# Another order for the loading phase of a fused cross-read and gated feed-forward kernel

## The chip, the cores and the metric

The kernel runs on one core of a Trainium2 chip. The metric is the device time of one execution in microseconds (us); the time of a kernel is the median of its runs. The names of the engines are those of the profile: PE is TensorE, DVE is VectorE, ACT is ScalarE, POOL is GpSimd, SP is SyncE. Each of them takes its own queue of instructions in order. DMAs are issued from the queues of POOL, SP and ACT, and 16 DMA engines carry them.

## What is computed

`x` has 8 batches, 8 heads, 512 tokens and 64 columns; `state` has 8 batches, 8 heads, 32 rows and 64 columns. Each reads the other by softmax attention; the results stand beneath each other, 544 tokens of 512 columns (the heads side by side) for each batch, and go through a gated feed-forward layer with 1536 inner columns:

```python
a = softmax(x @ state.T / 8)            # 512 x 32 for each head
xread = a @ state
a2 = softmax(state @ x.T / 8)           # 32 x 512 for each head
sread = a2 @ x
y = concat([xread, sread], axis=2)      # -> (8 * 544, 512), heads side by side
out = (sigmoid(y @ w_gate) * (y @ w_val)) @ w_out
```

Inputs and output are float32. The kernel multiplies in bfloat16 and sums in float32.

## The kernel before

**Algebra.** `xread @ w` is `a @ (state @ w)`, so the kernel never makes `xread`. For each batch it multiplies the 256 state rows (8 heads of 32) with the gate and value weights: `SW` (2 halves of 128 rows, gate and value, 1536 columns). Then `gv_mm(b, f)` (L340, its matmuls at L348) makes the gate and the value of 128 inner columns for the batch's 512 tokens: two matmuls each, `SW` times the transposed, normalised scores `aT`. `gv_th` (L354) is the tanh on ACT that stands for the sigmoid, `gv_glu` (L363) the product on DVE, `out_mm(b, k)` (L373, matmuls at L379) a third of the output product of 128 tokens. The `sread` rows of all batches are collected in `XS` and make a ninth, last "batch" of 256 rows.

**Scores.** `S_mm` multiplies transposed x (`xT`) with transposed state, `S_exp` is the exponential on ACT (the scores are small, no maximum is taken), `n_sum` and `n_mul` normalise half a batch on DVE, `n_sums` and `n_muls` a whole one (L159, L165). `aT` comes from PE for batches 0 and 1 (`aT_mm` L212, copied by `aT_cp`), from four DMA transposes on SP for the others (`aT_dma` L228). `xT` likewise: `xT_mm` (L110) with `xT_cp` on PE for batches 0 and 1, four DMA transposes (`at_xT_dma` L121) for the others, which read `xb`, the bfloat16 copy of x in another order that `cast_x` (L97) makes. `at_Eb` (L145) casts the exponentials on POOL for the `sread` side, and `sr_mm`, `sr_fin`, `p_tok`, `p_fold` make the `sread` rows of the first three batches.

**State.** `load_s(0)` brings the states of batches 0 and 1 in float32, `load_sb(q)` (L424) those of batches 2q and 2q+1 by a casting DMA, for q = 1 to 3. `sT_mm(q)` (L432) transposes them on PE: for q = 0 by eight matmuls with the identity into 64-row halves of the result, for q = 1 to 3 by eight matmuls with half the columns of the identity, one for each pair of an upper or lower half `e` and a quarter `l`. `sT_cp` brings the result to `sTc`, `sT_pad` and `pad` bring it beside zeros (`sTd`, `sTz`), the operand of `S_mm`.

**Weight products.** `sw_visit(b, lo, n, ...)` (L299, matmuls at L296) multiplies the state of batch b with n columns of the gate (0) or value (1) weights, of both where none is named; the results are copied from PSUM to `SW` by `sw_cp` (L334). `sw_wide` (L315) does 768 columns of both. The weights come by casting DMAs on POOL's queue, `load_w(w, lo, n)` (L85); the output weights in three thirds, `load_wo` (L93). x of batches 0 and 1 comes by casting DMAs in halves (`load_xh` L78), each in a tile of its own, of the others in float32 (`load_x`), into three rotating staging buffers `xf`.

**Order.** The schedule is manual: nothing but the order of the calls sets each engine's queue. Lines 462 to 707 are one hand-written list of calls, the loading phase. It begins with `warm` (L411, matmuls at L415), unread matmuls of the array of ones, 16 + 20 + 20 ahead of the first transposes and 12 later, of 128 columns each. Then it works off batches 0 and 1 as weights land, and what the steady loop needs of batch 2. From line 710 on the loop runs over b = 2 to 8: it does `gv_mm(b, f)` and `out_mm(b - 1, f)` in turn and, between them, the scores and weight products of batch b + 1, the first of which is `sw_wide(3, 0)`. The x of batch 3 is transposed at the end of the loading phase (`at_xT_dma(3)`), that of batch b + 2 in the loop, a batch ahead of its use. PSUM is divided into pools: two banks for `gvp`, one for `outp`, four for `swp`, one called `at`. A tile of a pool waits until the pool's oldest is read.

Of the kernel before, what the change touches and what calls it, by code (L numbers as in the profile page):

```python
# [16 lines left out]
def kernel(  # L17
# [43 lines left out]
    wo = wp.tile((128, NF, 512), BF, name="wo")  # L61
    sTd = wp.tile((128, 2, H, 2, Ns), BF, name="sTd")
# [102 lines left out]
    def n_muls(b, eng):  # L165
        abs_[b] = ap_.tile((128, 4, 2, 128), BF, name="ab")
        eng.tensor_tensor(abs_[b].rearrange("p c e (j n) -> p (c e j) n", n=Ns), E1s[b].rearrange("p c e j n -> p (c e j) n"),  # L167
# [37 lines left out]
    def n_mul(b, i, eng, lo=0, n=4):  # L205
# [3 lines left out]
        eng.tensor_tensor(abs_[b].rearrange("p c e (j n) -> p (c e) j n", n=Ns)[:, ce, 2 * i:2 * i + 2],  # L209
# [160 lines left out]
    def out_mm(b, k, place=None):  # L370
# [40 lines left out]
    def warm(n, place):  # L411

        ps = place[0].tile((128, 512), FP, name="warm", tag=place[1])
        for _ in range(n):
            nc.tensor.matmul(ps[:, :128], ones[:, 0], ones[:, 0], start=True, stop=True)  # L415
# [8 lines left out]
    def load_sb(q):  # L424
        sbs[q] = stg.tile((128, 1, 4, D), BF, name="sb", bufs=4)
        nc.gpsimd.dma_start(sbs[q][:, 0], state[2 * q:2 * q + 2].rearrange("b h (u l) d -> (b h u) l d", l=4))

    def cast_s(q, cp):
        sbs[q] = stg.tile((128, 1, 4, D), BF, name="sb", bufs=4)
        cp(sbs[q], sfs[q])  # L430

    def sT_mm(q, place):  # L432
        n = 128 if q == 0 else 64
        ps = stp[q] = place[0].tile((128, 4, n), FP, name="stp", tag=place[1])
        for l in range(4):
            for e in range(2):
                nc.tensor.matmul(ps[e * 64:(e + 1) * 64, l], sbs[q][:, 0, l], ident if q == 0 else ident_e[:, e],
                                 start=True, stop=True)
# [35 lines left out]
    xT_mm(0, 1, AT)
    sT_pad(0, vec)
    sT_pad(1, act)
    xT_cp(0, 0, vec)
    xT_cp(0, 1, vec)
    S_mm(0, 0, SWP, (0,))
    load_xh(1, 4, 4)  # L480
    S_mm(0, 0, SWP, (1,))
    S_exp(0, 0)
    load_xh(1, 0, 4)
    load_w(0, 256, 256)
    xT_mm(0, 3, AT)
    xT_cp(0, 3, vec)
    load_w(1, 256, 256)
    load_w(0, 1024, 512)
    n_sum(0, 0)
    xT_mm(0, 2, SWP)  # L490
    xT_cp(0, 2, act)
    warm(12, SWP)
    S_mm(0, 1, OU, (0,))
    load_w(1, 1024, 512)
    S_mm(0, 1, GV, (1,))
    S_exp(0, 1)
    xT_mm(1, 2, AT, 2)
    cast_x(0, pool, 2, 2)
    xT_cp(1, 2, act, 2)
    S_mm(1, 1, OU)  # L500
    xT_mm(1, 0, GV, 2)
    n_mul(0, 0, nc.vector)
    cast_x(0, act, 4, 2)
    n_sum(0, 1)
    n_mul(0, 1, nc.vector)
    cast_x(0, act, 6, 2)
    aT_mm(0, GV)
    xT_cp(1, 0, vec, 2)
    S_exp(1, 1)
    load_w(1, 0, 256)  # L510
    load_w(0, 0, 256)
    load_sb(1)
    S_mm(1, 0, AT)
    cast_x(0, act, 0, 2)
    aT_cp(0, 0, vec)
    sw_visit(1, 256, 256)
    aT_cp(0, 1, vec)
    S_exp(1, 0)
    sw_visit(0, 256, 256)
    sw_cp(0, 256, 2, 1, act)  # L520
    n_sums(1)
    at_Eb(0)
    sr_mm(0, AT)
    sw_cp(0, 256, 2, 0, act)
    sw_cp(1, 256, 2, 1, act)
    n_muls(1, nc.vector)
    gv_mm(0, 3, GV)
    sw_visit(0, 1024, 512, 0)
    sw_cp(1, 256, 2, 0, act)
    gv_th(0, 3)  # L530
    sw_visit(1, 1024, 512, 0)
    sw_cp(1, 1024, 0, 1, act)
    load_sb(3)
# [259 lines left out]
```

## Time and profile before

| what | value |
|---|---|
| median of 3 runs | 224.41 us (224.09 to 224.61) |
| the profiled execution | 224.35 us, of which the span of the profile is 222.6 |
| PE busy | 214.1 us, 96% of the span, 1895 matmuls |
| PE's weight loads (PEld, beside PE) | 110.0 us, 49% |
| DVE busy | 123.3 us, 55% |
| ACT busy | 129.5 us, 58% |
| POOL busy | 64.7 us, 29% |
| moved by DMA | 26.50 MB, 119 GB/s on average |

The span runs from the first to the last recorded instruction of the profiled execution; the execution's own time has a little more around it. Busy times are sums over the span. A line of the timeline gives the start in us, the time that a group of instructions took from its first to its last, the engine, the line, the operation and its tiles (out<-in), the shape, and in square brackets what the engine waited for ahead of the group. A row of the table of stretches gives the stretch, its length and how long each engine was busy in it (PE, PEld, DVE, ACT, POOL), with the granted clock and the use of the DMA engines behind. A line of DMA issues ends with the size and the time from issue to the last landing.

### The profile page before, as it was taken

What the parts mean: (1) busy time and instruction counts of PE and PEld (TensorE: products, weight loads), DVE (VectorE), ACT (ScalarE), POOL (GpSimd) and SP (SyncE); (2) the same over time, 40 slices, a digit from 0 to 9 for tenths busy, and PEclk for the clock granted to TensorE, in tenths of its full rate; (3) what the DMA queues carried; (4) which work ended last, traced back from release to release, by engine and by line L of the source; (5) the groups of instructions that cost most, each with busy time, mean ns of one, the idle gap of its engine ahead of it and who ended that gap; (6) DMA issues with size and microseconds to landing.
All of it is one profiled execution on the core that took longest, in us unless ns stands there. A gap on an engine that the chain in (4) does not pass through costs nothing.

```text
span 222.6 us, 4895 instructions
## 1 busy us (share of the span) xinstructions
PE 214.1 (96%) x1895; PEld 110.0 (49%) x1918; DVE 123.3 (55%) x214; ACT 129.5 (58%) x243; POOL 64.7 (29%) x122
## 2 busy tenths in 40 slices
PE   8878999999999999999999999999999999999994
PEld 8653344544444445444544454444444444466744
DVE  3599897977566445744484448354754334422301
ACT  2498886359575657656674866566756444433311
POOL 7988388570341036001800072003200000000001
DMA  6999999935695259724553305321132111211113
GB/s 95 179 206 258 232 168 166 276 51 142 155 311 164 52 138 249 183 44 147 161 121 85 115 0 120 107 70 42 50 80 70 49 47 57 75 59 49 47 33 111
DMA packets 40103, 26.50 MB, mean 119 GB/s; under 512 B 21936, under 2 KB 36144, under 8 KB 40080
## 3 DMA queue, kind: packets, MB, share of 16 engines
q1 hardware_dynamic: 30832, 17.80, 31.6%
q0 software_dynamic: 8960, 8.19, 21.1%
q8 instruction: 15, 0.25, 0.5%
q10 hardware_dynamic: 288, 0.20, 0.3%
q14 instruction: 8, 0.07, 0.1%
HBM read 18.35 MB, written 8.91 MB: 122 GB/s over the span
## 4 chain that ended last, share of the span: by engine, by line
PE 91%; DVE 5%; issue 1%; ACT 1%; DVEq 0%
PE outp L379 38%; PE gvp L348 36%; PE swp L296 5%; PE gvp L351 5%; PE warm L415 3%; PE Sp L137 1%; PE outp L401 1%; PE rdp L277 1%; DVE ab L167 1%; DVE ab L209 1%; DVE glu L363 1%; DVE rs L155 1%; PE aTp L216 1%; DVE rs L161 1%; DVE xT L119 0%
## 5 line engine op out<-in xcount | busy, mean ns | idle before, releaser
L363 DVE SCALAR_TENSOR_TENSOR glu<-th,gvp 128x512 bf16<-128x512 f32 (+1 forms) x108 | 70.1, 657 | 79.9 <-ACT th L358 64.4
L348 PE MATMUL gvp<-aT,SW 128*128 128x512 bf16 x384 | 96.7, 379 | 0.1
L379 PE MATMUL outp<-wo,glu 128*128 128x512 bf16 x373 | 95.4, 379 | 1.4 <-issue 0.3
L358 ACT ACTIVATE th<-gvp 128x512 f32<-128x512 f32 (+1 forms) x108 | 61.6, 576 | 56.6 <-PE gvp L348 43.2
L379 PEld LDWEIGHTS <-glu 128*128 128x128 bf16 x396 | 37.8, 98 | 42.2 <-issue 0.4
L348 PEld LDWEIGHTS <-SW 128*128 128x128 bf16 x384 | 36.1, 98 | 45.0 <-issue 3.9
L334 ACT CAST SW<-swp 128x512 bf16<-128x512 f32 x74 | 40.9, 586 | 5.4 <-PE swp L296 4.8
L383 ACT ACTIVATE res<-outp 128x512 f32<-128x512 f32 x33 | 19.7, 598 | 18.2 <-PE outp L379 18.1
L91 POOL COPY pre<-th 128x1 f32<-128x1 f32 x5 | 0.9, 187 | 73.4 <-ACT th L358 73.4
L392 POOL DMA_DIRECT2D out_dram<-res x2 | 1.1, 538 | 59.7 <-ACT res L383 59.7
L334 DVE CAST SW<-swp 128x512 bf16<-128x512 f32 x22 | 14.8, 684 | 2.5 <-PE swp L296 2.5
L148 POOL CAST Eb<-E 128x256 bf16<-128x256 f32 x32 | 11.4, 400 | 10.9 <-ACT E L142 10.8
L100 POOL CAST xb<-xf 128x1024 bf16<-128x1024 f32 x9 | 9.1, 1040 | 4.9 <-PE gvp L348 4.1
L142 ACT ACTIVATE E<-Sp 128x512 f32<-128x512 f32 x16 | 9.6, 604 | 1.5 <-PE Sp L135 1.2
L268 POOL CAST xs<-xf 128x1024 bf16<-128x1024 f32 x10 | 10.2, 1043 | 0.0
L209 DVE TENSOR_TENSOR ab<-E,ri 128x512 bf16<-128x512 f32 x12 | 9.0, 749 | 0.1
L296 PE MATMUL swp<-wg,sTc 64*32 64x512 bf16 (+1 forms) x192 | 8.6, 327 | 0.0
L155 DVE TENSOR_REDUCE rs<-E 128x16 f32<-128x512 f32 x12 | 8.1, 679 | 0.0
L415 PE MATMUL warm<-ones 128*128 128x128 bf16 x68 | 6.6, 286 | 1.0 <-DVE ones L461 1.0
L296 PE MATMUL swp<-wv,sTc 64*32 64x512 bf16 (+1 forms) x192 | 7.5, 322 | 0.0
L296 PEld LDWEIGHTS <-sTc 64*32 64x32 bf16 x384 | 4.8, 91 | 5.2 <-issue 3.0
L351 PE MATMUL gvp<-XS,wg 128*128 128x256 bf16 x48 | 7.2, 273 | 0.0
(83 smaller groups left out, 131.0 us busy)
## 6 DMA issues: line engine op xcount, KB each, us to landing
out_dram<-res SPq DMA_DIRECT2D x25, 256.0 KB, 2.7
xf<-in_x_dram SPq DMA_DIRECT2D x4, 1024.0 KB, 6.7
xf<-in_x_dram POOLq DMA_DIRECT2D x2, 1024.0 KB, 10.6
out_dram<-res SPq DMA_DIRECT2D x13, 128.0 KB, 2.0
wo<-in_moe_w_out_dram POOLq DMA_DIRECT2D x3, 512.0 KB, 9.3
xh<-in_x_dram POOLq DMA_DIRECT2D x4, 256.0 KB, 5.3
wg<-in_moe_w_gate_dram POOLq DMA_DIRECT2D x2, 512.0 KB, 10.3
wv<-in_moe_w_val_dram POOLq DMA_DIRECT2D x2, 512.0 KB, 11.5
```

Of the source, the lines that this page charges most:

```text
L148: nc.gpsimd.tensor_copy(Ebs[b][:, c], E1s[b][:, c])
L155: nc.vector.tensor_reduce(rs, halfE(b, i), AX.X, ALU.add)
L209: eng.tensor_tensor(abs_[b].rearrange("p c e (j n) -> p (c e) j n", n=Ns)[:, ce, 2 * i:2 * i + 2], halfE(b, i)[:, ce], ri[:, ce].unsqueeze ...
L296: nc.tensor.matmul(pss[e][j * Ns:(j + 1) * Ns, o:o + n], sTc[rows, b, j] if b > 1 else sTd[rows, b, 2 * j + e, e], (wg, wv)[w][rows, j, lo ...
L334: cp(*sw_left.pop((b, lo, w, e)))
L348: nc.tensor.matmul(ps, SWs[b][:, g, w, fs], aTs[b][:, :, g], start=(g == 0), stop=(g == 1))
L351: nc.tensor.matmul(ps, (wg, wv)[w][:, j, fs], XS[:, :, j], start=(j == 0), stop=(j == 3))
L358: nc.scalar.activation(th, held["gv", b, f][0], AF.Tanh, scale=0.5)
L363: nc.vector.scalar_tensor_tensor(glus[b][:, f], held["th", b, f], 1.0, held["gv", b, f][1], ALU.add, ALU.mult)
L379: nc.tensor.matmul(ops[b, c], glus[b][:, f, c * 128:(c + 1) * 128], wo[:, f], start=(f == 0), stop=(f == NF - 1))
L383: nc.scalar.activation(res, ops[b, c], AF.Copy, scale=0.5)
L415: nc.tensor.matmul(ps[:, :128], ones[:, 0], ones[:, 0], start=True, stop=True)
```

## The change

Only the loading phase and a few of its helpers are changed; of the steady loop only which results go out in two halves.

- **Unread matmuls.** `warm` now multiplies 512 columns at a time (the array of ones repeated four times). Ten of them stand ahead of the first transpose and two later: 12 of 512 columns in place of 68 of 128.
- **x of batches 0 and 1** comes into the staging buffers `xf`, padded to their size, in place of tiles of its own. The second halves of the heads are loaded and transposed first.
- **States of batches 2 to 7** come into `sbz`, where the 64 columns of each state piece stand between 64 zeros on each side (DVE writes the zeros once, ahead of the loads). A matmul whose 128 columns take the piece and the zeros ahead of it or behind it fills all 128 rows of the result, and two of them are added up in place of two that each write a half.
- **Order of the weights.** The columns 1024 to 1535 come first, then 256 to 511, 512 to 1023 and 0 to 255. The first weight products have 512 columns, and the first `gv_mm` is that of f = 11.
- **Normalisation.** The second half of batch 0 (`n_mul(0, 1)`) and all of batch 1 (`n_muls(1)`) are multiplied on POOL, in place of DVE.
- **Later loads.** x of batch 2 comes behind the last weight columns and states, x of batch 4 (on SP) is issued earlier than before, x of batch 3 (on POOL) later.
- **Order of the products.** All of batch 0's `gv_mm` now stand ahead of `S_mm(2)`, and `sw_wide(2, 0)` and `sw_wide(2, 1)` too, which before stood behind it.
- **Results.** `out_mm` sends six results in two halves as before, but others: rows (5, 2), (5, 3) and (6, 0) to (6, 3) of (batch, group) in place of (5, 0) to (5, 2) and (6, 0) to (6, 2).

The helpers:

```diff
+    sbz = wp.tile((128, 3, 9 * D), BF, name="sbz")
...
-            xhs[b] = wp.tile((128, H, 4, D), BF, name=f"xh{b}")
+            xhs[b] = stg.tile((128, H, 4, D), BF, name="xf", padded_shape=(128, 2 * H, 4, D))
...
+    def zero(t, eng):
+        (nc.gpsimd if eng is pool else nc.vector).memset(t, 0.0)
...
-                n = 256 if B - 4 < b < B - 1 and c < 3 else 512
+                n = 256 if 4 * (B - 1) - 6 <= 4 * b + c < 4 * (B - 1) else 512
...
-            nc.tensor.matmul(ps[:, :128], ones[:, 0], ones[:, 0], start=True, stop=True)
+            nc.tensor.matmul(ps.rearrange("p (r k) -> p r k", r=4), ones[:, 0], ones[:, 0].unsqueeze(1).to_broadcast((128, 4, 128)), start=True, stop=True)
...
     def load_sb(q):
-        sbs[q] = stg.tile((128, 1, 4, D), BF, name="sb", bufs=4)
-        nc.gpsimd.dma_start(sbs[q][:, 0], state[2 * q:2 * q + 2].rearrange("b h (u l) d -> (b h u) l d", l=4))
+        nc.gpsimd.dma_start(sbz[:, q - 1, D:].rearrange("p (l d) -> p l d", d=2 * D)[:, :, :D],
+                            state[2 * q:2 * q + 2].rearrange("b h (u l) d -> (b h u) l d", l=4))
...
-                nc.tensor.matmul(ps[e * 64:(e + 1) * 64, l], sbs[q][:, 0, l], ident if q == 0 else ident_e[:, e],
-                                 start=True, stop=True)
+                if q == 0:
+                    nc.tensor.matmul(ps[e * 64:(e + 1) * 64, l], sbs[q][:, 0, l], ident, start=True, stop=True)
+                else:
+                    lo = 2 * l * D + D - e * D
+                    nc.tensor.matmul(ps[:, l], sbz[:, q - 1, lo:lo + 2 * D], ident_e[:, e], start=(e == 0), stop=(e == 1))
```

The two orders, read along the lines, without the `sw_cp`, `gv_th`, `gv_glu`, `gate` calls, the ones of `pick` and the load of an activation table. Before:

```python
warm(16, AT); load_xh(0, 0, 4); load_s(0, nc.scalar); warm(20, SWP); load_xh(0, 4, 4); make_identity(nc, ident)
nc.vector.memset(sTd, 0.0); cast_s(0, vec); nc.vector.memset(sTz, 0.0); warm(20, SWP); sT_mm(0, OU); xT_mm(0, 0, SWP)
xT_mm(0, 1, AT); sT_pad(0, vec); sT_pad(1, act); xT_cp(0, 0, vec); xT_cp(0, 1, vec); S_mm(0, 0, SWP, (0,))
load_xh(1, 4, 4); S_mm(0, 0, SWP, (1,)); S_exp(0, 0); load_xh(1, 0, 4); load_w(0, 256, 256); xT_mm(0, 3, AT)
xT_cp(0, 3, vec); load_w(1, 256, 256); load_w(0, 1024, 512); n_sum(0, 0); xT_mm(0, 2, SWP); xT_cp(0, 2, act)
warm(12, SWP); S_mm(0, 1, OU, (0,)); load_w(1, 1024, 512); S_mm(0, 1, GV, (1,)); S_exp(0, 1); xT_mm(1, 2, AT, 2)
cast_x(0, pool, 2, 2); xT_cp(1, 2, act, 2); S_mm(1, 1, OU); xT_mm(1, 0, GV, 2); n_mul(0, 0, nc.vector)
cast_x(0, act, 4, 2); n_sum(0, 1); n_mul(0, 1, nc.vector); cast_x(0, act, 6, 2); aT_mm(0, GV); xT_cp(1, 0, vec, 2)
S_exp(1, 1); load_w(1, 0, 256); load_w(0, 0, 256); load_sb(1); S_mm(1, 0, AT); cast_x(0, act, 0, 2); aT_cp(0, 0, vec)
sw_visit(1, 256, 256); aT_cp(0, 1, vec); S_exp(1, 0); sw_visit(0, 256, 256); n_sums(1); at_Eb(0); sr_mm(0, AT)
n_muls(1, nc.vector); gv_mm(0, 3, GV); sw_visit(0, 1024, 512, 0); sw_visit(1, 1024, 512, 0); load_sb(3); aT_mm(1, OU)
load_x(2, nc.gpsimd); p_tok(1); gv_mm(0, 2, GV); sw_visit(1, 1024, 512, 1); aT_cp(1, None, vec); load_w(0, 512, 512)
sw_visit(0, 1024, 512, 1); gv_mm(1, 2, GV); cast_x(1, pool, 4, 2); gv_mm(1, 11, SWP); sr_fin(0); load_sb(2)
load_w(1, 512, 512); gv_mm(1, 8, SWP); gv_mm(0, 9, GV); sw_visit(0, 0, 256); gv_mm(0, 8, SWP); sw_visit(1, 0, 256)
cast_x(1, pool, 0, 2); gv_mm(1, 9, GV); gv_mm(0, 10, SWP); load_wo(0); cast_x(2, pool, 0, 4)
nc.gpsimd.memset(pick, 0.0); cast_x(2, vec, 4, 4); gv_mm(0, 1, SWP); gv_mm(0, 11, SWP); gv_mm(0, 0, GV); p_fold(1)
sT_mm(1, AT); sT_cp(1, act); sw_visit(1, 512, 512, 0); load_wo(1); sw_visit(0, 512, 512, 0); gv_mm(1, 0, GV)
sT_mm(3, AT); sT_mm(2, OU); sw_visit(0, 512, 512, 1); at_xT_dma(2); sw_visit(1, 512, 512, 1); sT_cp(2, vec)
gv_mm(1, 3, GV); gv_mm(0, 7, SWP); sT_cp(3, vec); load_wo(2); cast_x(1, pool, 2, 2); pad(2, 6); gv_mm(0, 5, SWP)
gv_mm(0, 4, SWP); load_x(3, nc.gpsimd); gv_mm(1, 4, SWP); gv_mm(0, 6, GV); at_Eb(1); S_mm(2, 0, SWP); S_mm(2, 1, OU)
gv_mm(1, 1, SWP); S_exp(2, 1); S_exp(2, 0); out_mm(0, 6, GV); n_sums(2); out_mm(0, 1, SWP); out_mm(0, 3)
cast_x(1, act, 6, 2); n_add(2); n_muls(2, nc.vector); out_mm(0, 0, SWP); out_mm(0, 2); at_Eb(2); aT_dma(2)
sr_mm(1, OU); out_mm(0, 4); out_mm(0, 5); sr_fin(1); out_mm(0, 8); sw_wide(2, 0); out_mm(0, 7, GV)
cast_x(3, vec, 0, 4); p_fold(2); sr_mm(2, SWP); gv_mm(1, 6, SWP); cast_x(3, act, 4, 4); sr_fin(2); at_xT_dma(3)
out_mm(0, 9); out_mm(0, 11); sw_wide(2, 1); out_mm(0, 10); gv_mm(1, 7, SWP); gv_mm(1, 10, SWP); gv_mm(1, 5, GV)
load_x(4, nc.sync)
```

After:

```python
warm(4, AT); zero(sTz, vec); zero(sTd, vec); warm(2, AT); warm(2, OU); warm(1, SWP); load_s(0, nc.scalar)
load_xh(0, 4, 4); load_xh(0, 0, 4); warm(1, AT); make_identity(nc, ident); xT_mm(0, 2, GV); cast_s(0, vec)
xT_cp(0, 2, vec); cast_x(0, act, 4, 2); xT_mm(0, 3, AT); xT_cp(0, 3, act); sT_mm(0, GV); sT_pad(1, act)
xT_mm(0, 0, OU); zero(sbz, vec); xT_mm(0, 1, SWP); xT_cp(0, 0, vec); xT_cp(0, 1, vec); sT_pad(0, act)
S_mm(0, 1, SWP, (0,)); load_xh(1, 4, 4); S_mm(0, 1, GV, (1,)); S_exp(0, 1); S_mm(0, 0, AT, (0,))
S_mm(0, 0, SWP, (1,)); warm(2, SWP); S_exp(0, 0); load_xh(1, 0, 4); load_w(0, 1024, 512); load_w(1, 1024, 512)
xT_mm(1, 2, SWP, 2); load_w(0, 256, 256); cast_x(0, act, 6, 2); load_w(1, 256, 256); xT_mm(1, 0, GV, 2); load_sb(1)
n_sum(0, 1); xT_cp(1, 2, vec, 2); S_mm(1, 1, SWP); xT_cp(1, 0, act, 2); load_w(0, 512, 512); S_mm(1, 0, GV)
S_exp(1, 1); n_sum(0, 0); n_mul(0, 0, vec); n_mul(0, 1, pool); cast_x(0, vec, 0, 2); aT_mm(0, OU); aT_cp(0, 1, vec)
aT_cp(0, 0, vec); sw_visit(0, 1024, 512, 0); S_exp(1, 0); sw_visit(1, 1024, 512, 0); load_sb(2); cast_x(0, pool, 2, 2)
at_Eb(0); sr_mm(0, OU); sw_visit(0, 1024, 512, 1); n_sums(1); load_w(1, 512, 512); sw_visit(1, 1024, 512, 1)
gv_mm(0, 11, GV); n_muls(1, pool); gv_mm(0, 9, SWP); gv_mm(0, 8, GV); sw_visit(1, 256, 256); sw_visit(0, 256, 256)
load_w(1, 0, 256); aT_mm(1, AT); sT_mm(1, GV); sT_cp(1, act); gv_mm(0, 10, SWP); gv_mm(0, 3, GV); aT_cp(1, None, vec)
gv_mm(1, 8, SWP); sr_fin(0); load_w(0, 0, 256); load_sb(3); gv_mm(1, 2, SWP); gv_mm(1, 11, SWP); gv_mm(1, 10, GV)
sT_mm(2, AT); load_x(2, nc.gpsimd); zero(pick, vec); load_wo(0); sw_visit(0, 512, 512, 1); sw_visit(0, 512, 512, 0)
load_wo(1); cast_x(1, pool, 2, 2); at_Eb(1); gv_mm(1, 3, GV); sw_visit(0, 0, 256); gv_mm(0, 5, SWP); load_wo(2)
gv_mm(0, 6, SWP); sT_cp(2, vec); p_tok(1); gv_mm(0, 4, GV); cast_x(1, pool, 0, 2); cast_x(2, pool, 0, 4)
gv_mm(0, 1, SWP); cast_x(1, vec, 4, 2); sT_mm(3, AT); cast_x(2, pool, 4, 4); sT_cp(3, act); gv_mm(0, 0, SWP)
at_xT_dma(2); gv_mm(0, 2, GV); gv_mm(0, 7, SWP); gv_mm(1, 9, GV); sw_wide(2, 0); out_mm(0, 1, GV); out_mm(0, 3)
sw_wide(2, 1); cast_x(1, vec, 6, 2); out_mm(0, 0, GV); out_mm(0, 2); load_x(4, nc.sync); sw_visit(1, 512, 512, 0)
sw_visit(1, 0, 256); pad(2, 6); out_mm(0, 4); sw_visit(1, 512, 512, 1); S_mm(2, 1, SWP); S_exp(2, 1); S_mm(2, 0, AT)
S_exp(2, 0); n_sums(2); p_fold(1); load_x(3, nc.gpsimd); out_mm(0, 5); at_Eb(2); out_mm(0, 6, OU); n_add(2)
out_mm(0, 8); out_mm(0, 10); gv_mm(1, 1, SWP); n_muls(2, vec); gv_mm(1, 0, GV); gv_mm(1, 6, SWP); sr_mm(1, AT)
sr_fin(1); out_mm(0, 7, SWP); cast_x(3, act, 0, 4); gv_mm(1, 4, SWP); aT_dma(2); p_fold(2); cast_x(3, act, 4, 4)
out_mm(0, 9); sr_mm(2, AT); at_xT_dma(3); gv_mm(1, 7, SWP); out_mm(0, 11); sr_fin(2); gv_mm(1, 5, GV)
```

More of the change, by code (lines that the diff above doesn't have):

```diff
@@ new lines @@
+    S_mm(1, 1, SWP)
+    xT_cp(1, 0, act, 2)
+    load_w(0, 512, 512)
+    S_mm(1, 0, GV)
+    S_exp(1, 1)
+    n_sum(0, 0)
+    n_mul(0, 0, vec)
+    n_mul(0, 1, pool)
+    cast_x(0, vec, 0, 2)
+    aT_mm(0, OU)
+    aT_cp(0, 1, vec)
+    aT_cp(0, 0, vec)
+    sw_visit(0, 1024, 512, 0)
+    sw_cp(0, 1024, 0, 1, vec)
+    S_exp(1, 0)
+    sw_visit(1, 1024, 512, 0)
+    sw_cp(1, 1024, 0, 1, act)
+    load_sb(2)
+    cast_x(0, pool, 2, 2)
+    sw_cp(1, 1024, 0, 0, act)
+    at_Eb(0)
+    sr_mm(0, OU)
@@ new lines @@
+    sw_cp(2, 1, 1, 0, act)
+    sw_cp(2, 1, 2, 0, vec)
+    sw_cp(2, 1, 1, 1, vec)
+    sw_visit(1, 512, 512, 0)
+    sw_cp(1, 512, 0, 1, vec)
+    sw_visit(1, 0, 256)
+    sw_cp(1, 0, 2, 1, act)
+    pad(2, 6)
+    sw_cp(2, 1, 0, 0, act)
+    out_mm(0, 4)
+    sw_visit(1, 512, 512, 1)
+    sw_cp(1, 0, 2, 0, vec)
+    S_mm(2, 1, SWP)
+    S_exp(2, 1)
+    S_mm(2, 0, AT)
+    S_exp(2, 0)
+    n_sums(2)
+    sw_cp(1, 512, 0, 0, act)
+    p_fold(1)
+    load_x(3, nc.gpsimd)
+    out_mm(0, 5)
+    at_Eb(2)
```

376 lines of the change are left out of this document (169 added, 207 removed).

## The prediction

> **What bounds the kernel now.** I read the page first (busy shares, then the chain), then the table of busy time by stretches, then the timeline of the first 30 us, then DMA issues, and last the SP queue around the entry to the steady loop.
>
> ```profile
> span 222.6 us, 4895 instructions
> ...
> PE 214.1 (96%) x1895; PEld 110.0 (49%) x1918; DVE 123.3 (55%) x214; ACT 129.5 (58%) x243; POOL 64.7 (29%) x122
> ...
> PE 91%; DVE 5%; issue 1%; ACT 1%; DVEq 0%
> ```
>
> TensorE is the bound. The table by stretches says where it is not yet:
>
> ```profile
> 10.00:15.00 5.00, 3.48 (x83) 2.55 (x83) 4.49 (x10) 4.23 (x9) 3.53 (x9) 1.00 1.32 200
> 15.00:20.00 5.00, 4.29 (x72) 2.22 (x72) 4.93 (x6) 4.65 (x9) 4.85 (x7) 1.00 1.35 200
> 20.00:25.00 5.00, 4.94 (x51) 1.92 (x36) 4.92 (x10) 4.09 (x8) 1.36 (x3) 1.00 1.15 300
> ```
>
> PE (second figure) fills its 5 us from 20 us on. From there to the end the waits of PE come to 0.3 us, and the steady loop is the same in both programs. So the change is worth what it does to the moment at which the loop's first weight products begin (`sw_wide(3, 0)`, 56.16 us in the timeline), and to the loop's first waits. The timeline of the loading phase:
>
> ```profile
> 1.04 5.75 PE L415 MATMUL warm<-ones 128*128 128x128 bf16 x56 [1.04 <-DVE ones L461]
> 6.72 0.41 PE L437 MATMUL stp<-ident,sb 128*64 128x128 bf16 x8
> 8.52 0.39 PE L135 MATMUL Sp<-sTd,xT 128*128 128x64 bf16 x8 [0.84 <-DVE xT L119]
> 12.08 0.41 PE L135 MATMUL Sp<-sTd,xT 128*128 128x64 bf16 x8 [1.15 <-ACT xT L119]
> 16.53 1.71 DVE L167 TENSOR_TENSOR ab<-E,ri 128x1024 bf16<-128x1024 f32 x1
> 18.30 0.62 PE L216 MATMUL aTp<-ident,ab 128*128 128x128 bf16 x8 [0.65 <-DVE ab L167]
> 20.27 3.89 PE L348 MATMUL gvp<-aT,SW 128*128 128x512 bf16 x16
> ```
>
> Unread matmuls hold PE until 6.8 although x's first half landed at 5.4 (issue 1.28 + 4.1). Then PE waits for copies on ACT and DVE, and at 18.30 for DVE's 1.71 us multiplication. The last of the four 512-column weight products (19.71) is followed by matmuls without a gap.
>
> **Ahead of the dense stretch.** The ten unread matmuls ahead of the first transpose have 512 columns: four times the 107 ns at which the first ones of 128 columns follow each other, 10 x 0.43 = 4.3 us, until 5.3. The first transposes then start when x lands, 5.4 against 6.72. The zeroing of `sbz` (864 words; sTz's 1024 took 0.91, so 0.8 on DVE) stands between two copies while x's second half is still on its way (7.5): nothing. Walking the queues with the rows' durations (S group 0.23, exp 0.60, xT copy 0.42 to 1.01, row sum 0.68, half multiplication 0.69) puts batch 1's exps at 11.7 and 12.2 against 12.95 and 14.26. That does not set the start any more, because the first weights are now 512 columns wide. The DMA answers for the two issues at 6.54 and 7.27, and the one at 17.11:
>
> ```profile
> wg<-in_moe_w_gate_dram POOLq DMA_DIRECT2D x1, 512.0 KB, 9.9
> wv<-in_moe_w_val_dram POOLq DMA_DIRECT2D x1, 512.0 KB, 11.7
> wg<-in_moe_w_gate_dram POOLq DMA_DIRECT2D x1, 512.0 KB, 10.6
> ```
>
> `wv` 1024 landed at 7.27 + 11.7 = 19.0. It now has two 256-column pieces fewer ahead. Those took 4.1 us of landings (x's last half at 10.2, second piece at 14.3), or by the 1.35 us between the later two (20.33, 21.67) only 2.7. So it lands at 14.9 to 16.3; I take the middle, 15.6. Behind it stand two value products of 0.56 each, and the first gate/value matmuls (`gv_mm(0, 11)`) start at 15.6 + 1.15 = 16.75. If it lands earlier, batch 0's `Eb` on POOL (half multiplication, DMA issue, cast 0.67, four casts 1.43) keeps `sr_mm(0)` in front and holds the start at 16.1.
>
> **How much work is left from there.** Before, 20.27 to 56.16 is 35.9 us of dense PE. By 20.27 it had done what the new order still has to do: two gv_mm (1.73), two 256-column visits (0.6), `aT_mm(1)` (0.45). Together 38.7, so the loop's products start at 16.75 + 38.7 = 55.45, 0.71 earlier. The states of batches 2 to 7 change nothing here: eight tiled matmuls took 0.25 (30.17 to 30.42) and sixteen 0.37; whole-array, 64 columns follow at 29 ns (sixteen Sp in 0.46), 3 x 0.23 = 0.69 against 0.62.
>
> The two multiplications on POOL: POOL's tensor_tensor took 0.73 for 256 columns and 0.45 for 64 partitions of 128, a line that gives 1.3 for 512 and 2.4 for 1024. DVE's took 0.69 or 0.95, and 1.22 or 1.71, the longer with POOL at work, so up to 1.4 times: 1.8 and 3.4. Batch 1's would run from 16.1 to 18.5 or 19.5; `aT_mm(1)` is due at 16.75 + 3.3 = 20.05. Hidden; below nothing it gives the 1.71 of DVE back, which the 38.7 contains.
>
> **Waits that the new order can add.** (a) *First 256 columns.* `sw_visit(0, 0, 256)` is due 11.0 us of PE work after the start, 27.75. Its weights now stand behind both pieces at 512. The old queue ran to 30.6 with the second of those; without x2 (2.95, now behind) and one state load (0.35) that is 27.3. Two `sbz` loads add their extra: 128-byte pieces in place of 512. Between 5 and 9 us, 1441 packets of 512 bytes are 44 ns per engine; the 420 packets of 1024 bytes between 15 and 17 us are 76. The line gives 14 to 17 ns for 128 bytes, 0.5 us a load against 0.35; if each costs as much as 512 bytes, 1.4. Nearest the line: 27.6, no wait; bound 1.65.
> (b) *xT of batch 2.* x2 lands at 31 instead of 25.3, two POOL casts of 1.04, then four transposes on SP issued from 33 to 38. Their last landing: 2.4 us after issue alone, 6.6 behind the weight queue (31.29 to 37.9): 39.1 to 43.3. `S_mm(2)` is due 25.6 after the start, 42.35. Nothing to 1; I take nothing.
> (c) *xT of batch 3.* The SP queue and PE around the loop's entry:
>
> ```profile
> 43.80 5.83 SPq L230 DMA_TRANSPOSE aT<-ab  x4
> 51.82 6.01 SPq L124 DMA_TRANSPOSE xT<-xb  x4
> 38.12 0.63 PE L137 MATMUL Sp<-sTz,xT 128*128 128x64 bf16 x16
> 60.40 0.40 PE L137 MATMUL Sp<-sTz,xT 128*128 128x64 bf16 x8
> ```
>
> Before, 22.3 us lie between batch 2's and batch 3's scores; now, counted off, 17.05. In it: exp, sums and multiplication 5.2 (before 5.7, with a glu between), four aT issues 5.1, four xT issues with the last landing 6.4: 16.7, just in time. One long issue (one of the four took 2.05 in the aT set, 2.16 in the xT set) makes 17.55, two 18.4. Nothing to 1.35; one long issue costs 0.5, I take half, 0.25.
> The early `load_x(4)` on SP (landing 6.7 us) is over before aT's issue at 48; x0's and x1's buffers are free by then; `load_x(3)` lands about 46, its casts are due at 52; the split results are six in both programs. Nothing; if x4 ran late it would show in (c).
>
> **The sum.** 224.35 (the profiled execution: span 222.6 and 1.75 around it, 0.06 below the runs' median) - 0.71 + 0.25 = 223.9.
>
> **Rivals.**
> *Given back on the queues (no change, 0.27).* wv at 16.2 (start 17.35, gain 0.11), or the middle value with two long issues (-0.71 + 1.35, or with one and part of (b)): 224.2 to 224.7. For it: 22.3 us of cover shrinks to 17. Against: later sets of four go without a long issue.
> *Small pieces (slower, 0.15).* Each `sbz` load at 1.4 us: w's first columns land at 29.4, PE waits 1.65, 224.35 - 0.71 + 1.65 + 0.25 = 225.5. It decides from 0.6 us a load and ends slower from 1.05 on. No row before has 128-byte pieces. [...]
> *The clock stays at half (slower, 0.10).* Matmuls of 128 columns follow at 107 ns until 6.2 us and at 56 after, though the table's granted clock says 1.00 throughout: the rate doubled after 5.1 us of unbroken matmuls. Now 4.3 unbroken ones are followed by transposes and gaps. If the rate is still low at the value products, those cost 0.9 more and the first gate/value matmuls 0.5: 224.35 - 0.71 + 0.25 + 1.4 = 225.3. [...]
> *POOL's multiplication (slower, 0.08).* At 5 us for 1024 columns, twice the line, `aT_mm(1)` waits 1.1: 225.0. DVE's factor was 1.4, not 2.
>
> **Numbers.** Forecast 223.9, chance 0.40, its own range 223.0 (start at 16.1, nothing in (c)) to 223.9. A measurement of this kernel can tell about 0.2%, 0.45 us, from no change. Faster by more 0.40, within 0.27, slower 0.15 + 0.10 + 0.08 = 0.33. The range 223.0 to 225.5 reaches to the slowest rival's time and leaves out only two of them together.
>
> **What would show it.** In the changed profile: transposes at 5.4; `gvp` without a gap from about 16.8; `wv`'s first piece landing near 15.6; `swp` of 256 columns near 27.8 without a wait on DMA; `stp` groups of 0.23; `Sp` of batch 3 near 59 with at most 0.3 us of wait; loop products at 55.5. A start after 17.4, a wait of over 0.5 us at the 256-column `swp` or at either `Sp`, or matmuls still 107 ns apart after 7 us makes it wrong.

## The result, and the profile after

The changed kernel took 224.94 us (median of 11 runs, 224.52 to 225.92); the kernel before, run with it, 224.11 us (median of 11 runs, 223.32 to 224.61). The ratio is 1.0040, 95% interval 1.0025 to 1.0056: slower by 0.9 us (0.0040 x 224.1) where I forecast faster by 0.45. The time lies inside the range, but it moved the other way. The profiled execution took 224.82 us, 223.0 of them the span.

The page of the changed kernel (the busy line, and of the 40 slices those of PE and of its granted clock; the page of before has no row PEclk, and its table of stretches shows 1.00 throughout):

```profile
span 223.0 us, 4792 instructions
...
PE 214.4 (96%) x1839; PEld 106.8 (48%) x1862; DVE 121.8 (55%) x214; ACT 130.1 (58%) x243; POOL 67.8 (30%) x123
...
PE   8689999999999999999999999999999999999994
...
PEclk9969999999999999999999999999999999999999
```

The table of stretches (after the stretch and its length: busy time of PE, PEld, DVE, ACT, POOL, then granted clock, DMA share, GB/s):

```profile
10.00:15.00 5.00, 3.13 (x48) 2.08 (x48) 4.93 (x9) 2.33 (x4) 4.61 (x8) 0.77 1.25 203
15.00:20.00 5.00, 5.00 (x68) 2.77 (x61) 4.58 (x7) 4.08 (x8) 2.98 (x4) 0.89 1.45 198
20.00:25.00 5.00, 4.99 (x66) 2.68 (x66) 4.78 (x10) 4.08 (x9) 5.00 (x9) 1.00 1.40 197
```

A clock of 0.77 and then 0.89 over 5 us each is 2 x (1.15 + 0.55) = 3.4 us at half speed. The timeline of PE shows which matmuls it met, and where PE waits later:

```profile
5.59 0.75 PE L120 MATMUL xTp<-ident,xf 128*128 128x128 bf16 x8
...
9.10 0.61 PE L120 MATMUL xTp<-ident,xf 128*128 128x128 bf16 x8
11.00 0.62 PE L120 MATMUL xTp<-ident,xf 128*128 128x128 bf16 x8 [1.29 <-DMA xf<-in_x_dram]
11.46 0.40 PE L139 MATMUL Sp<-sTd,xT 128*128 128x64 bf16 x8
12.73 0.61 PE L139 MATMUL Sp<-sTd,xT 128*128 128x64 bf16 x8 [0.87 <-ACT xT L123]
13.15 1.04 PE L220 MATMUL aTp<-ident,ab 128*128 128x128 bf16 x8
14.12 1.05 PE L300 MATMUL swp<-wg,sTd 64*32 64x512 bf16 x16
15.13 1.01 PE L251 MATMUL srp<-Eb,ones 128*128 128x128 bf16 x8
...
17.20 2.84 PE L352 MATMUL gvp<-aT,SW 128*128 128x512 bf16 x12
...
43.22 0.66 PE L141 MATMUL Sp<-sTz,xT 128*128 128x64 bf16 x16
...
53.41 0.22 PE L246 MATMUL srp<-hl,pick 128*128 128x128 bf16 x1 [0.38 <-POOL hl L198]
...
56.61 0.41 PE L300 MATMUL swp<-wg,sTc 64*32 64x512 bf16 x8
...
60.89 0.40 PE L141 MATMUL Sp<-sTz,xT 128*128 128x64 bf16 x8
```

The transposes begin at 5.59 (forecast 5.4). The eight `aTp` transposes took 1.04 us (0.62 before), the sixteen gate products 1.05 (0.63 in other runs): these ran at the half clock. The first gate/value product starts at 17.20 (forecast 16.75). At 53.41 PE waits for `hl`. The bracket counts 0.38 us of it, from the end of the last matmul; but matmuls of 512 columns follow each other at 0.22 us and are shown to end 0.38 us after their start, so the next one could have started 0.16 us ahead of that end, and 0.54 us are lost. Where the text below gives a wait without a bracket, it is this lost time. The loop's products start at 56.61 in place of 56.16; from there to the end of the span there are 166.4 us in both kernels. So the loss between the two profiled executions is the entry into the loop, 0.45 us later, and nothing behind it.

What stands behind the wait at 53.41 is told by the chain of waits (start, us, what), and SP's queue shows the other chain that starts at the same scores:

```profile
43.24 0.42 PE Sp L141 x8
...
43.74 1.09 ACT E L146 x2
...
44.86 1.23 DVE rs L165
...
47.60 1.15 POOL F L187
...
53.41 0.22 PE srp L246
```

```profile
48.67 5.76 SPq L234 DMA_TRANSPOSE aT<-ab  x4
54.54 5.14 SPq L128 DMA_TRANSPOSE xT<-xb  x4
```

`p_fold(2)` on POOL runs from 47.60 to 53.37 and starts from batch 2's scores, by way of the exponentials, sums and `n_add`. On SP the transposes of batch 3's x end with a landing 2.5 us behind the last issue (58.41), at 60.90, when the scores of batch 3 begin (60.89).

### The profile page after: what moved, and what is told of

Read it like the earlier page. It is cut to its first block, busy times and chain, and to the rows that moved or that the text cites. A ratio compares the mean times of both kernels' runs of the same rounds, so it can differ in the third digit from the quotient of the medians.

```text
span 223.0 us, 4792 instructions
## 1 busy us (share of the span) xinstructions
PE 214.4 (96%) x1839; PEld 106.8 (48%) x1862; DVE 121.8 (55%) x214; ACT 130.1 (58%) x243; POOL 67.8 (30%) x123
## 4 chain that ended last, share of the span: by engine, by line
PE 88%; POOL 3%; DMA 3%; issue 2%; DVE 1%; ACT 1%; POOLq 0%; ACTq 0%
PE gvp L352 36%; PE outp L383 36%; PE swp L300 6%; PE gvp L355 5%; DMA xf<-in_x_dram 3%; PE Sp L141 1%; PE outp L405 1%; POOL xf L84 1%; PE rdp L281 1%; POOL F L187 1%; PE aTp L220 1%; DVE rs L165 1%; POOL F L192 1%; ACT E L146 0%; ACT xT L123 0%
## 5 line engine op out<-in xcount | busy, mean ns | idle before, releaser
L104 POOL CAST xb<-xf 128x1024 bf16<-128x1024 f32 x10 | 10.2, 1045 | 1.9 <-DMA xf<-in_x_dram 1.9
L272 POOL CAST xs<-xf 128x1024 bf16<-128x1024 f32 x10 | 10.2, 1044 | 0.0
L213 DVE TENSOR_TENSOR ab<-E,ri 128x512 bf16<-128x512 f32 x11 | 7.8, 706 | 0.0
L355 PE MATMUL gvp<-XS,wv 128*128 128x256 bf16 x48 | 7.2, 273 | 0.0
```

The source lines that it names most:

```text
L104: cp(xbs[b].rearrange("p c h d -> p h c d")[:, lo:lo + n], (xhs if b in xhs else xfs)[b][:, lo:lo + n])
L272: pool(xs.rearrange("p c h d -> p h c d")[:, lo:lo + n, :, :D], xfs[b][:, lo:lo + n])
L355: nc.tensor.matmul(ps, (wg, wv)[w][:, j, fs], XS[:, :, j], start=(j == 0), stop=(j == 3))
```

## The experiments

Four groups, each run with the kernel before, whose median was 224.23, 224.05, 224.32 and 224.39 us. These medians of one and the same kernel differ by 0.34 us, 0.0015, so all comparisons are by the ratio to the kernel before. The difference of two ratios has an uncertainty of about 0.002; smaller differences are hints. The table:

| kernel | edits | median us | ratio | 95% interval |
|---|---|---|---|---|
| changed kernel | | 224.94 | 1.0040 | 1.0025 to 1.0056 |
| e1_fill | more unread matmuls | 224.74 | 1.0021 | 1.0005 to 1.0038 |
| e2_pick_last | `hl` read last | 224.88 | 1.0033 | 1.0013 to 1.0052 |
| e3_pick_s3later | `hl` last, batch 3's scores later | 224.64 | 1.0020 | 1.0001 to 1.0039 |
| e4_all | e1 and e3, x of batch 2 earlier | 224.94 | 1.0032 | 1.0012 to 1.0053 |
| e5_slack | e1 and e3, `rd_dma(3)` later | 224.38 | 1.0009 | 0.9996 to 1.0021 |
| e6_before_slack | before, with e3 and `rd_dma(3)` later | 224.17 | 1.0008 | 0.9996 to 1.0020 |
| e7_mul_dve | e1, multiplications on DVE | 225.23 | 1.0055 | 1.0039 to 1.0070 |
| e8_states | e1, states as before | 225.12 | 1.0039 | 1.0025 to 1.0052 |
| e9_rd | e1, `rd_dma(3)` later | 224.57 | 1.0018 | 1.0007 to 1.0030 |
| e10_no_rd | e1 and e3 | 224.51 | 1.0007 | 0.9994 to 1.0019 |
| e11_start | e5, one cast on ACT | 223.91 | 0.9980 | 0.9968 to 0.9991 |
| e12_before_extra | before, one more transpose | 225.13 | 1.0033 | 1.0019 to 1.0047 |
| e13_cast_only | the cast on ACT alone | 224.84 | 1.0019 | 1.0009 to 1.0029 |
| e14_no_fill | e11 without e1's matmuls | 224.05 | 0.9991 | 0.9977 to 1.0004 |
| e15_no_room | e1 and the cast on ACT | 224.46 | 1.0008 | 0.9997 to 1.0019 |

### The clock: e1_fill

```diff
     xT_mm(1, 2, SWP, 2)
+    warm(4, OU)
...
     S_mm(1, 1, SWP)
+    warm(2, OU)
```

> The changed kernel with six more unread matmuls of 512 columns in PE's idle time between 9.5 and 12.7 us (four behind the transposes of batch 1's second half, two behind the first scores of batch 1). Clock theory (the half clock from 12.7 to 16.1 us is where the time went): the granted clock stays 1.00, the first gate/value matmuls start near 16.75 us in place of 17.2, and the time falls by the 0.45 us, to 224.5. Latency theory (the x of batch 2 lands at 31.0 us, and from there a chain of copies and DMA transposes sets the scores of batches 2 and 3, whatever PE does): the clock stays 1.00 and the start is 16.75, but the scores of batch 2 still wait for xT, which lands last at 43.3, and the time stays within 0.2 us of 224.94.

Measured: 1.0021, and the granted clock was full (0.998 or more) in all 12 executions. In the changed kernel 7 of 11 executions had 0.992, which is what 3.4 us at half speed make of a span of 223 us; their mean is 225.28 us, that of the other four 224.78. Over all variants of the changed kernel without the six extra matmuls it was 0.992 or less in 28 of 59 executions, with them 2 of 92; in the five kernels without them, the executions with the half clock took 0.2 to 0.8 us longer on average than the others. The timeline of PE:

```profile
9.38 1.03 PE L419 MATMUL warm<-ones 128*128 128x512 bf16 x4
...
12.17 0.41 PE L139 MATMUL Sp<-sTd,xT 128*128 128x64 bf16 x8 [0.44 <-ACT xT L123]
12.45 0.60 PE L220 MATMUL aTp<-ident,ab 128*128 128x128 bf16 x8
12.98 0.62 PE L300 MATMUL swp<-wg,sTd 64*32 64x512 bf16 x16
14.76 0.61 PE L251 MATMUL srp<-Eb,ones 128*128 128x128 bf16 x8 [1.15 <-DVE aT L230]
...
16.32 3.12 PE L352 MATMUL gvp<-aT,SW 128*128 128x512 bf16 x12
```

The products take 0.62 again. The clock theory was right in this: with the idle time between 9.5 and 12.7 us the clock falls in about half of the executions, with matmuls in it in 2 of 92. By the ratios it explains about 0.4 us of 0.9, not all. The start gained only part of what PE gained, since now `sr_mm` waits 1.15 us for DVE's copies of `aT`, a wait that no forecast named.

Three kept traces hold a stretch at half clock. In the changed kernel, the 3.4 us ahead of the fall and the 3.4 us behind it:

```profile
9.31:12.73 3.42, 1.26 (x25) 0.97 (x22) 3.32 (x7) 1.99 (x4) 2.51 (x4) 1.00 1.25 197
12.73:16.14 3.41, 3.41 (x44) 2.38 (x45) 3.41 (x5) 1.93 (x4) 2.50 (x6) 0.50 1.32 201
```

Ahead of the fall in e13 and in e7 (both told below), and a stretch of e3, whose clock stays full to the end:

```profile
9.94:13.36 3.42, 1.58 (x32) 1.28 (x30) 2.94 (x6) 2.31 (x5) 2.61 (x3) 1.00 1.24 205
```

```profile
4.42:7.84 3.42, 1.68 (x19) 0.80 (x17) 1.20 (x2) 2.08 (x4) 3.42 (x5) 1.00 1.27 156
```

```profile
9.45:12.86 3.41, 1.23 (x24) 0.94 (x21) 3.31 (x7) 1.95 (x4) 2.46 (x4) 1.00 1.23 192
```

Ahead of each fall PE had been busy for 1.26 to 1.68 of 3.4 us. The longest single wait does not decide: e3 kept its clock through one of 1.31 us, e13 lost it with none above 0.97 in that stretch. Nor does the least work in just any 3.4 us: e3 had 1.23. Why only some executions lose the clock is not shown.

### The entry into the loop: e2_pick_last, e3_pick_s3later, e4_all

e2 moves one matmul in `sr_mm`, so that the other sixteen stand ahead of the wait:

```diff
         if ("hl", b) in held:
-            nc.tensor.matmul(sm, pick, held["hl", b], start=True, stop=True)
             terms = []
...
                                  Eb[:, c, :, j], start=(c == 0), stop=(c == 3))
+        if ("hl", b) in held:
+            nc.tensor.matmul(sm, pick, held["hl", b], start=True, stop=True)
```

> The changed kernel, but sr_mm of batches 1 and 2 does the one matmul that reads hl (the result of p_fold on POOL) behind its other sixteen matmuls, which cover 0.47 us. Fold theory (PE's wait of 0.38 us and more at 53.4 us for hl is lost time): the wait is gone and the time falls by 0.45 us, to 224.5. Latency theory: the wait at 53.4 goes, but the four DMA transposes of batch 3's x still land last at 60.9 us, so PE waits there for its scores instead, 0.4 us or more, and the time stays within 0.2 us of 224.94.

Measured: 1.0033, which cannot be told from the 1.0040 of the changed kernel. The timeline shows where a gain could go:

```profile
60.49 0.25 PE L141 MATMUL Sp<-sTz,xT 128*128 128x64 bf16 x3
61.02 0.32 PE L141 MATMUL Sp<-sTz,xT 128*128 128x64 bf16 x5 [0.28 <-DMA xT<-xb]
```

The loop's products started at 56.21, 0.40 us earlier than in the changed kernel. (This execution had the full clock and its first gate/value product 0.34 us earlier, at 16.86, but it lost the same 0.34 us among the first of these products; so the 0.40 are the wait for `hl`, less 0.15 at batch 2's scores.) But batch 3's scores then lost 0.45 us behind their third matmul until the last transpose of x landed (60.98). The wait for `hl` had hidden the wait for x. This is what the latency theory said.

e3 adds 1.73 us of room to it:

```diff
-                if f in (1, 2):
-                    S_mm(nb, f - 1, AT)
-                    S_exp(nb, f - 1)
+                g = f - (nb == 3)
+                if g in (1, 2):
+                    S_mm(nb, g - 1, AT)
+                    S_exp(nb, g - 1)
...
```

(the sums, the multiplication and the cast that follow use g too)

> As the run before, and the scores of batch 3 with what follows from them stand one step (1.73 us of PE work) later in the loop. Latency theory: both waits at the loop's entry are gone, those that the trace of the changed kernel shows (0.5 us) and those that other executions of it have when one or two transposes on SP issue late (up to 0.7 us more): 224.3 or less. Clock theory: only the 0.45 us of the hl wait goes, 224.5; the half clock stays in most runs. Rival (the steady loop needs batch 3's scores where they were): a new wait of up to 1.7 us at batch 3's aT, 225 or more.

Measured: 1.0020, with neither wait in the trace; 5 of 12 executions had the half clock. By the medians half of the loss is gone, 0.0020; e2, with only the wait for `hl` removed, got back 0.0007.

e4 puts e1 and e3 together, moves `load_x(2)` ahead of `load_w(1, 0, 256)` and `sw_visit(0, 0, 256)` behind `gv_mm(0, 4)`, and puts the gate/value products that follow in another order.

> Both edits of the run before, the six more unread matmuls, and x of batch 2 loaded ahead of the weight columns 0 to 255 (with batch 0's products of these columns behind four more of its gate/value products). Latency theory: x of batch 2 lands near 28 us in place of 31, its xT near 40, the scores of batch 2 do not wait; with the start at 16.75 the loop's products start near 55.4 as predicted, and the time is 223.6 to 223.9. Clock theory and fold theory: their shares add up to the same 223.9, but then the first run is 0.45 below the changed kernel and the second too. If the loss lies elsewhere (small DMA pieces, POOL's multiplication, order of the products): 224.5 or more.

Measured: 1.0032, a clear miss. x of batch 2 landed at 28.07 in place of 31.0, but its casts stand behind other work of POOL. The transposes were issued from 31.45 on and landed by 42.99, beside the loads of the output weights: 0.3 us earlier than in the changed kernel. The trace shows new waits, 0.26 us at batch 4's scores among them. e10_no_rd, below, is this kernel without the moved load and the new order, and took 1.0007 in another group: the two together did harm. Which of them, and why so much, was not settled.

### Room further on: e5_slack, e6_before_slack, e9_rd, e10_no_rd, e12_before_extra

```diff
                 if f == 6:
                     aT_dma(nb)
-                    rd_dma(nb)
+                    if nb > 3:
+                        rd_dma(nb)
...
                     at_xT_dma(nb + 1)
+                    if nb == 3:
+                        rd_dma(nb)
```

> The changed kernel with everything that could wait at the loop's entry given room, and x of batch 2 loaded where the change has it: six more unread matmuls, the matmul that reads hl last, the scores of batch 3 one step later, and the SP queue's transpose of batch 3's sread rows behind the four transposes of batch 4's x (that takes 1.2 us out of the chain to batch 4's scores, for which the traces show 0.1 to 0.5 us of room in the changed kernel and its variants, 1.0 before). Theory of the room (the scores of batches 3 and 4 wait in most executions because the chain of DMA transposes has lost its room): no waits are left but those at the first gate/value products, and the time is 224.2 to 224.3, level with the kernel before. Theory of more work (the new order has 0.6 us more on PE between the first gate/value product and the loop than I counted, and that alone takes the gain away): the median stays at 224.6 to 224.7.

> Control: the kernel before with the same three edits behind the loop's entry (the matmul that reads hl last, the scores of batch 3 one step later, the transpose of batch 3's sread rows behind those of batch 4's x). Both theories: no change within 0.2 us of 224.23, since its trace has no wait at any of these places and 1.0 us of room at batch 4's scores. If it gains more than 0.3 us, then the room was short before too, and the loss of room does not tell the two kernels apart.

Measured: e5 1.0009, the control 1.0008; neither can be told from the kernel before. So the six matmuls and the room take back most of the loss, and the same room gives the kernel before nothing. "More work on PE" alone, the rival, would have left e5 at 1.002 or more, the edge of its interval. Which room it is:

> The changed kernel with the six more unread matmuls and, of the edits behind the loop's entry, only one: the transpose of batch 3's sread rows on SP stands behind the four transposes of batch 4's x. If the room at batch 4's scores is what most executions lack: 1.0010 of the kernel before, as with all edits (1.0009). If the room at batch 3's scores is: 1.0020, as with the unread matmuls alone. If each has a part: about 1.0015.

> The complement: the unread matmuls, the matmul that reads hl last and the scores of batch 3 one step later, with the transpose of batch 3's sread rows where it was. Batch 3's scores have 1.7 us more room, batch 4's 0.5 us less (the aT of batch 3 is issued 0.6 us later). If the room at batch 4's scores decides: 1.0020 or more. If that at batch 3's decides: 1.0010.

Measured: e9 1.0018, e10 1.0007. By the medians the room at batch 4's scores alone gives nothing, and that at batch 3's scores, with `hl` last, gives what there is, even though e10's own trace has batch 4's scores waiting 0.36 us. The two intervals overlap, so this is a hint and not shown.

For e12, `nc.sync.dma_start_transpose` of `xr` into a spare tile was added to the kernel before, behind `rd_dma(3)`.

> The kernel before with one more DMA transpose on SP, of the same size as the one of batch 3's sread rows and into an unused tile, ahead of the transposes of batch 4's x: it takes 1.2 us out of 1.0 us of room there. Theory of the room: batch 4's scores wait 0.2 us or more in most executions, the time rises by 0.2 to 0.5 us to 224.4 or 224.7, with no other change. If the chain of SP has more room than the landing in one trace shows: no change.

Measured: 1.0033, the median 0.8 us above the kernel before, more than forecast. In its trace batch 4's scores wait 0.28 us, and 0.4 us more lie behind the last matmul of the span, which the theory does not explain. If it is the chain of SP that the extra transpose lengthens, before had no more than about 1 us of room there; the exact price stays open.

### The states and the multiplications: e7_mul_dve, e8_states

```diff
-    n_mul(0, 1, pool)
+    n_mul(0, 1, vec)
...
-    n_muls(1, pool)
+    n_muls(1, vec)
```

> The changed kernel with the six more unread matmuls and both multiplications back from POOL to DVE. On POOL the first took 1.05 us and stands ahead of the casts of Eb, which hold sr_mm of batch 0 and with it the first gate/value product. If that sets the start: sr_mm starts 0.4 to 0.8 us earlier, the first gate/value product at 16.2 to 16.4 in place of 16.3 to 16.9, and the time falls by 0.2 to 0.4 against 224.74. If DVE's 0.9 us ahead of batch 0's transposes and 1.7 us ahead of the copies of the first products weigh more: slower by 0.3 to 1 us. If the landing of the value weights (15.3 to 16.1) sets the start: within 0.2.

Measured: 1.0055 against e1's 1.0021. Its first gate/value product starts at 17.70, and DVE, with the multiplications back, keeps a later one waiting:

```profile
20.95 0.59 PE L352 MATMUL gvp<-aT,SW 128*128 128x512 bf16 x2 [0.63 <-DVE glu L367]
```

POOL is the better place for them. (The profiled execution also had 3.4 us of half clock, from 7.84 on, which delays its start too; the other five did not, and took 225.17 us on average.)

e8 brings the states as before (no `sbz`, tiles of their own, eight 64-row matmuls).

> The changed kernel with the six more unread matmuls, and the states of batches 2 to 7 as before: 512-byte pieces in a tile without zeros, eight 64-row matmuls each. The rival of small pieces (each state load costs 1.4 us on the queue in place of 0.35): every load behind the first state load lands 1 us earlier and the time falls by 0.5 us or more against 224.74. Otherwise, by the trace of the changed kernel (a state load lands 0.46 us behind the one ahead of it; 24 matmuls took 0.79 us in place of 0.62): 0.1 us faster, which is within the noise.

Measured: 1.0039, not faster; against e1's 1.0021 the intervals overlap. In its trace x of batch 2 lands at 30.95, as with the small pieces (30.72 in e1). So the small pieces cost nothing that the kernel sees.

### The start: e11_start, e13_cast_only, e14_no_fill, e15_no_room

```diff
-    cast_x(0, vec, 0, 2)
...
     S_exp(1, 0)
+    cast_x(0, act, 0, 2)
```

> The version with all the room (six unread matmuls, hl last, batch 3's scores later, the sread transpose later) with the cast of batch 0's heads 0 and 1 on ACT in place of DVE, where it took 1.73 us beside POOL's casts and held the copies of batch 0's aT and so sr_mm. If that sets the start: sr_mm of batch 0 starts near 14.4 in place of 14.8 to 15.3, the first gate/value product at 16.2 to 16.5, the time falls by 0.2 to 0.4, to 0.999 to 1.000 of the kernel before. If the value weights set it (landing 15.3 to 16.1): within 0.1 us, 1.001.

Measured: 0.9980, interval 0.9968 to 0.9991. This version beats both kernels. (The two orders printed ahead of the prediction show that the kernel before has this cast on ACT too.) DVE's queue of the changed kernel, the same cast on ACT in e11, and PE's start in e11:

```profile
12.55 1.73 DVE L104 COPY xb<-xf 128x512 bf16<-128x512 bf16 x1
14.23 0.76 DVE L230 COPY aT<-aTp 128x512 bf16<-128x512 bf16 x2
```

```profile
13.08 0.61 ACT L104 COPY xb<-xf 128x512 bf16<-128x512 bf16 x1
```

```profile
14.27 0.64 PE L250 MATMUL srp<-Eb,ones 128*128 128x128 bf16 x8 [0.38 <-DVE aT L230]
...
16.01 2.95 PE L353 MATMUL gvp<-aT,SW 128*128 128x512 bf16 x12
```

The wait of `sr_mm` falls from 1.15 us in e1 to 0.38, the first gate/value product comes 0.3 to 0.9 us earlier than in e1 to e5. The cast cost DVE 1.73 us and costs ACT 0.61.

The last group takes the three parts apart:

> The changed kernel with nothing but the cast of batch 0's heads 0 and 1 on ACT in place of DVE. If the start is worth its 0.3 to 0.7 us by itself: 1.001 to 1.002 of the kernel before (the changed kernel: 1.004). If the waits for xT of batch 2 (landing 43 us), for hl and for xT of batch 3 eat it, and the half clock stays: 1.003 to 1.004.

> The best version (0.998) without the six more unread matmuls. If the half clock costs 0.5 us in the executions that have it, about half of them: 0.999 to 1.000, with a granted clock of 0.992 in about half of the executions. If the start no longer hangs on PE there: 0.998.

> The best version without the edits behind the loop's entry: unread matmuls and the cast on ACT alone. If the room at batch 3's scores and the wait for hl are worth 0.3 us and more where PE comes earlier: 1.000 or more. If the earlier start does without: 0.998 to 0.999.

Measured: 1.0019, 0.9991 and 1.0008. Two steps are larger than the uncertainty of 0.002 and stand within one group too: the cast beside the rest (0.0029 from e5 to e11; 0.6 us from e10 to e11, which differ in `rd_dma(3)` too), and the room beside the cast (0.0028 from e13 to e14). The extra matmuls are not clear by the ratios (0.0019 alone, 0.0011 from e14 to e11), but within e14 the three executions with the half clock took 224.71 us on average, the other nine 223.90. The cast alone is not shown to help: the ratio falls from 1.0040 to 1.0019, but the medians from 224.94 to 224.84 only, and e13's profiled execution, with the half clock, starts at 17.27 and enters the loop at 56.70, no earlier than the changed kernel. All three together are 0.006, 1.3 us.

That this is also what lay between my forecast (0.998 of the kernel before) and the changed kernel (1.004) is chance, since the forecast knew none of the three edits. So is it that e14's profiled execution enters the loop at 55.39 us, where the forecast said 55.45: it starts 0.5 us earlier than the forecast and takes 0.5 us longer from there.

## Why the prediction was wrong

Three steps failed: that the clock holds through the gaps at the start, that the first products wait for `wv` or POOL and not for DVE, and the list of waits at the loop's entry, which lacked `hl`. That the time still lies in the range is luck: the range reached up to 225.5 for the rival of the small pieces, which did not come.

**The start, 16.75.** With the full clock it was 16.3 to 16.9 in e1 to e4, but 16.75 was right by two errors that cancel. I counted the two value products behind `wv` at 0.56 each; 0.56 is what both took together (19.71 to 20.27 before). With that the sum would have been 15.6 + 0.56 = 16.2. Against it, `wv` landed at 16.04, within the 14.9 to 16.3 of the forecast but later than the value taken, and `sr_mm` waited for DVE.

**The clock.** The step that failed is that the clock, once up, stays up; "the clock stays at half" was a rival with 0.10. That PE would run at half the rate near the start of the dense stretch was right, the form and the price were not. The rate did double at 5.9 us (matmuls of 128 columns 107 ns apart, then 56), and fell again at 12.7, after 3.4 us with 1.26 us of PE work, 1.02 of it transposes. What ran at half speed was `aTp`, the gate products and the first part of `sr_mm`, not the value products, and the price was about 0.5 us, not 1.4: e3, whose `wv` landed at 16.09 and whose clock was full, started at 16.71, the profiled execution at 17.20. The sign that I had named came: matmuls of 128 columns were 107 ns apart again from 13.2 us on. I had looked at a gap of 1.3 us in the profile of before (PE's wait ahead of 12.08, 1.15 by its bracket), behind which eight transposes took 0.61 us, the full rate, and taken the clock for safe. What I did not add up is that before, twelve unread matmuls (0.67 us) and one more group of scores stood in the same stretch. What in that stretch makes the clock fall, and only in some executions, no run shows. That the twelve matmuls kept it up before was not tested; e1's six come nearest to it.

**What held the start.** I named `Eb` on POOL as the bound behind `wv`. It was DVE: the cast that the new order puts there takes 1.73 us beside POOL's copy and casts, and the copies of `aT` stand behind it. The sum had no term for that cast. With the rest of the edits in place, moving it off DVE was worth about 0.6 us (e11).

**Work left, 38.7.** 38.9 in the profiled execution (39.41 less the wait of 0.54 for `hl`); 39.36 in e3, which starts earlier and loses 0.35 us among the first gate/value products; these wait, as far as the order tells, for the copies of the first `SW` pieces. That wait the forecast left out. The 24 state matmuls took 0.79, not 0.69.

**Waits (a), (b), (c).** (a) The first 256 columns landed at 27.66 (forecast 27.6), no wait; in e5 and e11, where they came at 28.41 and 27.82 and PE was early, about 0.46. (b) The last xT of batch 2 landed at 43.28, the far end of 39.1 to 43.3, and its scores began at 43.22: no room left, as in the forecast's bound and not in its value. (c) Counted right, one long issue and all: 5.76 and 5.14 us on SP, landing at 60.9. Priced at 0.25, it cost 0.45 in e2 and was hidden by another wait in the changed kernel.

**The wait that was not in the list.** `hl`: 0.54 us. `p_fold(2)` needs 5.8 us on POOL from `n_add`, 10.2 from batch 2's scores. Before, 10.5 us of PE work lay between these scores and `sr_mm(2)`, and `hl` was done at 48.46, 0.16 us ahead of its use; now 9.7 lie there. I had followed one chain from these scores, to SP, and not the other, to POOL.

**The sum.** 55.45 + 0.45 (later start) + 0.54 (`hl`) + 0.17 (work) = 56.61, the measured start of the loop's products. That is 1.16 us later than forecast; less the 0.25 that stood in the sum for (c), it gives 0.91, and the profiled execution took 224.82 us against the 223.9 of the forecast. The medians differ by more than the profiled executions (0.83 against 0.47 us); this is scatter between executions, and which waits make it is not shown.

**The other rivals.** POOL's multiplications took 1.05 and 1.91 us, below the 1.3 and 2.4 of the line; no loss, and DVE would be worse (e7). Small pieces: a load of states landed 0.46 us behind its forerunner (0.5 by the prediction; the 44 and 76 ns that it names give 20 ns for 128 bytes, and with that 0.65); the bound of 1.4 is excluded. "Given back on the queues" had the right kind of place but was taken for no change, 224.2 to 224.7. Its second case does not even add up to that: 224.35 - 0.71 + 1.35 = 224.99, which is slower than no change and near the measured 224.94. In the trace it was not two long issues that made the time, but the half clock and `hl`.

## What to carry to other kernels

Where a change puts PE's work in another order, the work that covered other chains can get shorter (here 10.5 to 9.7 us, and 22.3 to 17.1). List every chain that starts from the same event (here the scores of one batch: one to SP, one to POOL) with its length and its cover, before and after, and treat a tie as a loss, since executions of one kernel differ by half a microsecond and more (those of before lay between 223.32 and 224.61). Removing the wait that a trace shows may only uncover the next: e2 gained less than 0.2 us, which is within the noise, by removing a wait of 0.54. Where matmuls wait for data at the start, do not take the clock for safe by the longest gap alone: here it fell behind 3.4 us with 1.26 to 1.68 us of PE work, in e13 with no wait above 0.97, and six more unread matmuls kept it up in 90 of 92 executions. And redo each term of a sum on the lines that it was read from: here the value products, counted twice, made the start come out right for a wrong reason.

## What the runs showed of the hardware

- The granted clock fell to half for 3.4 us after stretches of the same length in which PE was busy for 1.26, 1.58 and 1.68 us (three traces), with no single wait above 1.32 us; e3 kept it through 1.23 us of work and a wait of 1.31. In the five kernels without the six further unread matmuls a granted clock of 0.992 or less came in 28 of 59 executions. With six unread matmuls of 512 columns (1.3 us) between 9.4 and 12.7 us it was 0.998 or more in 90 of 92.
- The same DVE copy (128x512, bfloat16 to bfloat16) comes three times in the trace of the changed kernel and took 1.73 us at 12.55, beside POOL's copy of the same kind (0.90 at 12.19) and its four casts of `Eb` (1.48 at 13.04), 0.60 at 31.70, beside two POOL casts from float32 (2.08 at 31.12), and 0.28 at 38.80, beside small operations of POOL (128x128: 0.45 at 38.37, 0.35 at 38.88). The longest is six times the shortest. Whether it is POOL's work that makes the difference, and by what, no run shows.
